# A gated mix of a state-space convolution and a Fourier filter: one of the sine products moves to GpSimd, its sign is turned back at an eviction, and responses are stored eight channels at a time

## The chip, the cores and the metric

One core of a Trainium2 chip runs the whole kernel in one launch. The metric is the device time of that launch in microseconds; the median of three runs stands for the kernel. The profile shows one further execution, instruction by instruction.

## The reference

The input x has 2048 positions and 640 channels. Branch A is a long convolution: each channel has a response K of 2048 values, a sum over 128 decaying complex exponentials, and the convolution is done with transforms of twice the length. Branch B filters the same x with a two-dimensional real Fourier transform. A sigmoid gate mixes them.

```python
def _A_ref(u, log_A_real, A_imag, C_real, C_imag, log_dt, D_skip):
    dt = jnp.exp(log_dt)
    A = -jnp.exp(log_A_real) + 1j * A_imag
    C = (C_real + 1j * C_imag) * dt[:, None]
    P = jnp.exp((A * dt[:, None])[:, :, None] * pos[None, None, :])
    K = 2.0 * jnp.einsum("dn,dnl->dl", C, P).real
    ...                                   # y = irfft(rfft(u, 2L) * rfft(K, 2L))[:L]
    return y + u * D_skip[None, None, :]

def _B_ref(x, w_r, w_i):
    X = jnp.fft.rfft2(x, axes=(-2, -1))
    X = X * (w_r + 1j * w_i)
    return jnp.fft.irfft2(X, s=(S, D), axes=(-2, -1))

g = sigmoid((x * gate_w).sum(-1, keepdims=True))
return g * _A_ref(...) + (1 - g) * _B_ref(...)
```

## The kernel before

Two streams of work are written side by side by `merge` and then ordered for each engine by a scheduler; on an engine the order is fixed before the launch, and each engine runs its own list in order, waiting on semaphores. The first stream (`phase_a`) transforms x along the positions (lines L335, L348, until about 160 us), then does the Fourier filter of branch B, called FNet below: nine blocks of rows, each of which goes through `front` (tiles ue, fo, fg), transposes (p_t), matmuls (p_d), the filter `filt` on VectorE (tiles xx, mm, zz, pm) and two back transforms (p_eo, p_i). After it `phase_c` starts the transform of the responses, `first`.

The second stream is `phase_b`. It makes the responses K, in 40 tiles of 16 channels (four blocks of 40 groups of four channels). For a tile t:

- `mags` makes e, the magnitudes: three matmuls p_e (L638) and three exponentials on ScalarE (L640), 128 x 1536.
- `phases` makes q, the angles, 128 x 1024: two matmuls p_p (L649), a copy on ScalarE (L651) and a subtraction on VectorE (L652). The first 512 of them belong to x, the last 512 to y.
- `trig` takes the magnitude of the angles, aq (VectorE, L662), and four sines on ScalarE: sc holds both of y's, in SBUF; sx and cx are x's sine and cosine, in PSUM.
- `prods` multiplies. x[:, 1] is e times sx, near half (32 positions, L676) and far half with a minus sign (L675); x[:, 0] is e times cx for both halves (L677, 1024 wide). All three run on VectorE and read e from SBUF and the sines from PSUM. y's two products (L679, L680) run on GpSimd and read SBUF alone, the only memory that GpSimd works on here.
- `kgen` multiplies y by x on TensorE: 32 small matmuls p_k (L693). After every second tile the eight channels in p_k are copied by ScalarE into kt (L701); after ten tiles one store takes kt's 40 columns to k_d (L703).

Exponentials and sines come in turns of five tiles (BT = 5), since ScalarE changes its tables between them. I call the stretches Exp stage and Sin stage; there are eight of each. Tiles q, aq and sc come from one pool of five buffers, b_w; sx and cx have one PSUM bank each. `prods(t)` is written behind `trig(t + 1)`, and `kgen(t)` some two tiles later. A buffer's next writer waits for the last reader of what it held.

The transformed x goes to DRAM (u_d) from ut, a pool of four, and FNet reads it back (ue). Stores and loads on SP, ScalarE's queue (ACTq) and GpSimd are issued in order on each of them. `first` (L750 and the copy it hands to `stage1`) reads k_d back and transforms it; `phase_d` multiplies, transforms back and writes out, from about 438 us on.

Of the kernel before, what the change touches and what calls it, by code (L numbers as in the profile page):

```python
# [9 lines left out]
F32 = mybir.dt.float32  # L10
# [3 lines left out]
ALU = mybir.AluOpType  # L14
# [36 lines left out]
def _tables():  # L51
# [19 lines left out]
    for r in range(4):  # L71
# [5 lines left out]
        np.full((128, 1), HALF_PI)], 1)  # L77
# [106 lines left out]
def body(tc, A, out):  # L184
    nc = tc.nc
    T = Ctx()
    with ExitStack() as top:
# [19 lines left out]
        T.sg = [take(1), take(1)]  # L207
        T.hpi = take(1)
# [392 lines left out]
def phase_b(tc, A, T, ctx):  # L601
# [5 lines left out]
    wt = ctx.enter_context(tc.tile_pool(name="b_w", reuse_waits="tile", bufs=5))  # L607
# [5 lines left out]
    pt = ctx.enter_context(tc.tile_pool(name="b_pt", reuse_waits="tile", bufs=1, space=PSUM))  # L613
# [41 lines left out]
    def trig(t, r):  # L655

        aq = wt.tile([128, 2, 16, 32], F32, tag="w", name="aq")
        sc = r.sc = wt.tile([128, 2, 16, 32], F32, tag="w", name="sc")
        sx, cx = r.sx, r.cx = [pt.tile([128, 16, 32], F32, tag=n, name=n) for n in ("sx", "cx")]
        fl = lambda t: t.rearrange("p d i -> p (d i)")  # L660
        af = aq.rearrange("p v d i -> p (v d i)")
        V.tensor_scalar(out=af.bitcast(I32), in0=r.q.bitcast(I32), scalar1=0x7FFFFFFF, scalar2=None, op0=ALU.bitwise_and)  # L662

        with after(st.exp):
            S.activation(fl(sc[:, 0]), r.q[:, 512:1024], AF.Sin, scale=TWO_PI)  # L665
        S.activation(fl(sc[:, 1]), af[:, 512:1024], AF.Sin, scale=-TWO_PI, bias=T.hpi)  # L666
        S.activation(fl(sx), r.q[:, 0:512], AF.Sin, scale=TWO_PI)
        T.trig = st.trig = S.activation(fl(cx), af[:, 0:512], AF.Sin, scale=-TWO_PI, bias=T.hpi)  # L668

    def prods(t, r):  # L670
        e, sx, cx, sc = es[t], r.sx, r.cx, r.sc
        x = wk.tile([128, 2, 16, 64], F32, tag="x", name="x")
        y = wk.tile([128, 2, 16, 32], F32, tag="y", name="y")
        xy[t] = (x, y)
        V.scalar_tensor_tensor(out=x[:, 1, :, 32:64], in0=e[:, :, 32:64], scalar=-1.0, in1=sx[:, :, :], op0=ALU.mult, op1=ALU.mult)  # L675
        V.tensor_tensor(out=x[:, 1, :, 0:32], in0=e[:, :, 0:32], in1=sx[:, :, :], op=ALU.mult)  # L676
        V.tensor_tensor(out=x[:, 0].rearrange("p d (h j) -> p d h j", h=2), in0=e[:, :, 0:64].rearrange("p d (h j) -> p d h j", h=2),  # L677
                        in1=cx.unsqueeze(2).broadcast_to([128, 16, 2, 32]), op=ALU.mult)
        G.tensor_tensor(out=y[:, 1], in0=e[:, :, 64:96], in1=sc[:, 0], op=ALU.mult)  # L679
        G.tensor_tensor(out=y[:, 0], in0=e[:, :, 64:96], in1=sc[:, 1], op=ALU.mult)  # L680

    def kgen(t):
        x, y = xy.pop(t)
        if t % 10 == 0:
            st.kt = w1.tile([128, 40, 64], F32, tag="k", name="kt")
        kt = st.kt
# [47 lines left out]
def phase_c(tc, A, T, ctx):  # L734
# [243 lines left out]
```

## Time and profile before

| | us |
|---|---|
| median of three runs | 609.23 (608.76 to 611.23) |
| the profiled execution's own time | 608.74 |
| its span, first to last instruction | 607.0 |
| TensorE busy | 535.8 (88%) |
| VectorE busy | 500.2 (82%) |
| ScalarE busy | 364.8 (60%) |
| GpSimd busy | 267.0 (44%) |

By stretches of the span, busy us of each engine:

| stretch | TensorE | VectorE | ScalarE | GpSimd |
|---|---|---|---|---|
| 0 to 53: first transforms of x, parameters | 43.49 | 34.95 | 28.90 | 28.88 |
| 53 to 160: more of them, beside ten tiles of responses | 98.07 | 78.69 | 73.29 | 33.44 |
| 160 to 438: FNet beside thirty tiles | 249.45 | 251.59 | 220.80 | 121.56 |
| 438 to 607: products with the responses, output | 144.81 | 134.97 | 41.85 | 83.11 |

A row of the profile names the line of the kernel, the engine (PE is TensorE, DVE VectorE, ACT ScalarE, POOL GpSimd, SPq SyncE's queue), the operation and the tiles, out<-in. Busy time is the time in which an engine had an instruction in work; a recorded instruction can contain waiting for the memory port.

### The profile page before, as it was taken

What the parts mean: (1) busy time and instruction counts of PE and PEld (TensorE: products, weight loads), DVE (VectorE), ACT (ScalarE), POOL (GpSimd) and SP (SyncE); (2) the same over time, 40 slices, a digit from 0 to 9 for tenths busy, and PEclk for the clock granted to TensorE, in tenths of its full rate; (3) what the DMA queues carried; (4) which work ended last, traced back from release to release, by engine and by line L of the source; (5) the groups of instructions that cost most, each with busy time, mean ns of one, the idle gap of its engine ahead of it and who ended that gap; (6) DMA issues with size and microseconds to landing.
All of it is one profiled execution on the core that took longest, in us unless ns stands there. A gap on an engine that the chain in (4) does not pass through costs nothing.

```text
span 607.0 us, 16654 instructions
## 1 busy us (share of the span) xinstructions
PE 535.8 (88%) x7084; PEld 405.6 (67%) x7084; DVE 500.2 (82%) x748; ACT 364.8 (60%) x659; POOL 267.0 (44%) x246
## 2 busy tenths in 40 slices
PE   9688979989968989989798999898989999999874
PEld 7576657766656657676566676565878877787631
DVE  5971597598899989999999899979399796987974
ACT  4556775576846876888589888799723332231210
POOL 4931252053525344454326335416254347547441
PEclk9899989989989996998899999999999999999998
DMA  8787204245612320332250233006685989889776
GB/s 341 293 288 268 79 5 151 69 154 181 239 43 67 97 87 13 108 118 109 67 151 12 75 97 110 24 28 200 224 346 184 356 273 299 291 271 310 225 231 239
DMA packets 48083, 101.98 MB, mean 168 GB/s; under 512 B 3316, under 2 KB 32776, under 8 KB 46248
## 3 DMA queue, kind: packets, MB, share of 16 engines
q1 hardware_dynamic: 24888, 67.74, 32.3%
q10 hardware_dynamic: 20080, 22.52, 11.9%
q0 software_dynamic: 3040, 10.65, 5.3%
q8 instruction: 56, 0.92, 0.6%
q14 instruction: 19, 0.16, 0.1%
HBM read 60.91 MB, written 39.98 MB: 166 GB/s over the span
## 4 chain that ended last, share of the span: by engine, by line
PE 51%; DVE 27%; ACT 9%; DMA 8%; issue 4%; POOL 1%; ACTq 0%; DVEq 0%; POOLq 0%; SPq 0%
PE p_eo L551 8%; PE p_s L348 8%; PE p_s L335 6%; PE p_e L638 5%; PE p_k L693 4%; PE p_i L814 4%; PE p_p L649 3%; DVE q L652 3%; PE p_d L518 2%; DVE t L801 2%; PE p_i L565 2%; PE p_t L502 2%; DVE ma L795 2%; PE p_c L893 2%; PE p_d L519 2%
## 5 line engine op out<-in xcount | busy, mean ns | idle before, releaser
L679 POOL TENSOR_TENSOR y<-e,sc 128x512 f32<-128x512 f32 x40 | 56.7, 1418 | 131.0 <-ACT sc L665 60.3
L348 PE MATMUL p_s<-t,w 128*64 128x160 f32 x1056 | 92.4, 314 | 10.2 <-ACT ut L382 5.1
L348 PEld LDWEIGHTS p_s<-t,w 128*64 128x64 f32 x1056 | 76.5, 139 | 21.4 <-ACT ut L382 6.0
L640 ACT ACTIVATE e<-p_e 128x512 f32<-128x512 f32 x120 | 68.6, 602 | 22.7 <-PE p_e L638 20.4
L551 PE MATMUL p_eo<-td,pmt 107*128 107x321 f32 x204 | 69.0, 459 | 3.9 <-ACT pmt L505 3.9
L693 PE MATMUL p_k<-x,y 128*32 128x64 f32 x2560 | 63.6, 229 | 9.8 <-DVE x L677 2.9
L693 PEld LDWEIGHTS p_k<-x,y 128*32 128x32 f32 x2560 | 46.1, 113 | 38.0 <-issue 29.4
L652 DVE SCALAR_TENSOR_TENSOR q<-q,p_p 128x512 f32<-128x512 f32 x80 | 53.4, 681 | 13.5 <-ACT q L651 11.8
L336 ACT COPY t<-p_s 128x512 f32<-128x512 f32 x40 | 24.6, 623 | 65.2 <-PE p_s L335 41.8
L638 PE MATMUL p_e<-rm,par 128*128 128x512 f32 x120 | 58.7, 519 | 3.4 <-ACT e L640 2.8
L680 POOL TENSOR_TENSOR y<-e,sc 128x512 f32<-128x512 f32 x40 | 54.5, 1362 | 6.5 <-ACT sc L666 6.5
L800 POOL TENSOR_TENSOR t<-ma 64x320 f32<-64x320 f32 x32 | 28.0, 875 | 61.4 <-DVE ma L795 51.8
L551 PEld LDWEIGHTS p_eo<-td,pmt 107*128 107x128 f32 x204 | 38.4, 198 | 19.6 <-ACT pmt L505 6.9
L677 DVE TENSOR_TENSOR x<-e,cx 128x1024 f32<-128x1024 f32 x40 | 48.6, 1214 | 2.2 <-ACT cx L668 2.2
L651 ACT ACTIVATE q<-p_p 128x512 f32<-128x512 f32 x80 | 46.5, 592 | 4.2 <-PE p_p L649 3.8
L649 PE MATMUL p_p<-rp,par 128*128 128x512 f32 x80 | 43.5, 548 | 4.5 <-DVE q L652 4.5
L814 PE MATMUL p_i<-t,w 128*64 128x160 f32 x528 | 42.7, 300 | 4.4 <-POOL t L801 3.4
L335 PE MATMUL p_s<-c,kt 128*64 128x128 f32 x640 | 43.0, 274 | 3.9 <-DVE mb L796 2.0
L335 PEld LDWEIGHTS p_s<-c,kt 128*64 128x64 f32 x640 | 38.0, 136 | 12.6 <-issue 7.7
L816 ACT COPY s<-p_i 128x640 f32<-128x640 f32 x32 | 21.8, 694 | 40.0 <-PE p_i L814 30.4
L335 PE MATMUL p_s<-c,u 128*64 128x128 f32 x640 | 41.5, 278 | 2.5 <-ACT ut L382 2.5
L795 DVE TENSOR_TENSOR ma<-p_s,us 128x640 f32<-128x640 f32 (+1 forms) x36 | 28.2, 784 | 18.8 <-PE p_s L348 11.5
(153 smaller groups left out, 1181.5 us busy)
## 6 DMA issues: line engine op xcount, KB each, us to landing
u_d<-ut SPq DMA_DIRECT2D x32, 320.0 KB, 2.6
us<-u_d ACTq DMA_DIRECT2D x16, 640.0 KB, 6.0
s_d<-s ACTq DMA_DIRECT2D x15, 640.0 KB, 8.3
t<-s_d SPq DMA_DIRECT2D x14, 640.0 KB, 5.9
ww<-in_w_l SPq DMA_DIRECT2D x8, 642.0 KB, 4.0
ue<-u_d SPq DMA_DIRECT2D x8, 640.0 KB, 4.4
k_d<-kt SPq DMA_DIRECT2D x4, 1280.0 KB, 7.6
kt<-k_d SPq DMA_DIRECT2D x8, 640.0 KB, 5.9
```

Source lines behind the costliest of these rows:

```text
L335: nc.tensor.matmul(p[64 * ri:64 * ri + 64, j, :], src(i + j), e1[ri], start=True, stop=True)
L348: ins = nc.tensor.matmul(p[64 * j:64 * j + 64, i, 160 * ri:160 * ri + 160], w2[:, x, 64 * ri:64 * ri + 64], t1[:, x // 2 if x < 32 else K0 ...
L551: P.matmul(p[:, :E], st.pmt[:DC, c, w, j, :], tv[:DC, w, c, :], start=c == 0, stop=c == 2)
L638: P.matmul(p[:, :], pars[t], rm[:, c:c + 512], start=True, stop=True)
L640: st.exp = S.activation(ef[:, c:c + 512], p[:, :], AF.Exp)
L649: P.matmul(p[:, :], pars[t], rp[:, c:c + 512], start=True, stop=True)
L652: V.scalar_tensor_tensor(out=qf[:, c:c + 512], in0=qf[:, c:c + 512], scalar=MAGIC, in1=p[:, :], op0=ALU.subtract, op1=ALU.subtract)
L677: V.tensor_tensor(out=x[:, 0].rearrange("p d (h j) -> p d h j", h=2), in0=e[:, :, 0:64].rearrange("p d (h j) -> p d h j", h=2), in1=cx.uns ...
L679: G.tensor_tensor(out=y[:, 1], in0=e[:, :, 64:96], in1=sc[:, 0], op=ALU.mult)
L680: G.tensor_tensor(out=y[:, 0], in0=e[:, :, 64:96], in1=sc[:, 1], op=ALU.mult)
L693: P.matmul(st.pb[32 * r:32 * r + 32, o, :], y[:, ri, 4 * qq + JR[r], :], x[:, ri, 4 * qq + JR[r], :], start=t % 2 + qq + 1 - ri == 0, stop ...
L814: T.mm = P.matmul(p[x:x + 64, i // 2, 160 * (i % 2):160 * (i % 2) + 160], T.w3[:, k0 + h + i, x:x + 64], t2[:, h + i, :], start=True, stop ...
```

## The change

x's two halves trade engines and signs. Its product with the sine, x[:, 1], is now one operation of 1024 elements on GpSimd, without the minus sign; its product with the cosine, x[:, 0], is two operations of 512 on VectorE, the far half with a minus sign. The response of the far half therefore comes out negated, and `near` turns it back: the eviction in `first` on ScalarE multiplies by T.sa, a column of 1 and -1. Since GpSimd reads no PSUM here, the sine must lie in SBUF: the sines are written over the angles (q) and over their magnitudes (aq), in place, and sc and sx go away. So all four sines come behind aq, which reads q; before, the two that read q directly did not. The pool b_w has six buffers, two for a tile in place of three; cx has two PSUM banks. kt holds eight columns, has two buffers, and is stored after every second tile: 20 stores of 512 columns in place of four of 2560.

```diff
@@ -74,7 +74,7 @@
     c1 = np.concatenate([
         e1[0], e1[1], e3.reshape(4, 32, 64).swapaxes(0, 1).reshape(128, 64), e3e.reshape(128, 128), np.eye(128), one,
         np.repeat([-1.0, 1.0], 64)[:, None], np.repeat([1.0, -1.0], 64)[:, None],
-        np.full((128, 1), HALF_PI)], 1)
+        np.tile(np.repeat([1.0, -1.0], 32), 2)[:, None], np.full((128, 1), HALF_PI)], 1)
 
     k = np.array(POS_K)
     a = np.arange(64)
@@ -205,6 +205,7 @@
         T.e1 = [take(128), take(128)]
         T.e3, T.e3e, T.id, T.one = take(64), take(128), take(128), take(32)
         T.sg = [take(1), take(1)]
+        T.sa = take(1)
         T.hpi = take(1)
         T.w2 = cst.tile([128, NP, 128], F32, name="w2")
         T.gate = cst.tile([128, 2, 16], F32, name="gate")
@@ -604,13 +605,13 @@
     V, G, S, P = nc.vector, nc.gpsimd, nc.scalar, nc.tensor
     BT = 5
     ep = ctx.enter_context(tc.tile_pool(name="b_e", reuse_waits="tile", bufs=BT))
-    wt = ctx.enter_context(tc.tile_pool(name="b_w", reuse_waits="tile", bufs=5))
+    wt = ctx.enter_context(tc.tile_pool(name="b_w", reuse_waits="tile", bufs=6))
     wk = ctx.enter_context(tc.tile_pool(name="b_x", reuse_waits="tile", bufs=3))
     w2 = ctx.enter_context(tc.tile_pool(name="b_p", reuse_waits="tile", bufs=2))
     w1 = ctx.enter_context(tc.tile_pool(name="b_k", reuse_waits="tile", bufs=1))
     ps = ctx.enter_context(tc.tile_pool(name="b_ps", reuse_waits="tile", bufs=2, space=PSUM))
     pk = ctx.enter_context(tc.tile_pool(name="b_pk", reuse_waits="tile", bufs=1, space=PSUM))
-    pt = ctx.enter_context(tc.tile_pool(name="b_pt", reuse_waits="tile", bufs=1, space=PSUM))
+    pt = ctx.enter_context(tc.tile_pool(name="b_pt", reuse_waits="tile", bufs=2, space=PSUM))
     rp, rm = T.rp, T.rm
     dsk = w1.tile([128, 4, 40], F32, name="dsk")
     V.memset(dsk[:, :, :], 0.0)
@@ -654,36 +655,33 @@
 
     def trig(t, r):
 
-        aq = wt.tile([128, 2, 16, 32], F32, tag="w", name="aq")
-        sc = r.sc = wt.tile([128, 2, 16, 32], F32, tag="w", name="sc")
-        sx, cx = r.sx, r.cx = [pt.tile([128, 16, 32], F32, tag=n, name=n) for n in ("sx", "cx")]
+        aq = r.aq = wt.tile([128, 2, 16, 32], F32, tag="w", name="aq")
+        cx = r.cx = pt.tile([128, 16, 32], F32, tag="cx", name="cx")
         fl = lambda t: t.rearrange("p d i -> p (d i)")
         af = aq.rearrange("p v d i -> p (v d i)")
         V.tensor_scalar(out=af.bitcast(I32), in0=r.q.bitcast(I32), scalar1=0x7FFFFFFF, scalar2=None, op0=ALU.bitwise_and)
-
         with after(st.exp):
-            S.activation(fl(sc[:, 0]), r.q[:, 512:1024], AF.Sin, scale=TWO_PI)
-        S.activation(fl(sc[:, 1]), af[:, 512:1024], AF.Sin, scale=-TWO_PI, bias=T.hpi)
-        S.activation(fl(sx), r.q[:, 0:512], AF.Sin, scale=TWO_PI)
-        T.trig = st.trig = S.activation(fl(cx), af[:, 0:512], AF.Sin, scale=-TWO_PI, bias=T.hpi)
+            S.activation(r.q[:, 512:1024], r.q[:, 512:1024], AF.Sin, scale=TWO_PI)
+        S.activation(r.q[:, 0:512], r.q[:, 0:512], AF.Sin, scale=TWO_PI)
+        S.activation(fl(cx), af[:, 0:512], AF.Sin, scale=-TWO_PI, bias=T.hpi)
+        T.trig = st.trig = S.activation(af[:, 512:1024], af[:, 512:1024], AF.Sin, scale=-TWO_PI, bias=T.hpi)
 
     def prods(t, r):
-        e, sx, cx, sc = es[t], r.sx, r.cx, r.sc
+        e, cx = es[t], r.cx
+        si = r.q.rearrange("p (v d i) -> p v d i", v=2, d=16)
         x = wk.tile([128, 2, 16, 64], F32, tag="x", name="x")
         y = wk.tile([128, 2, 16, 32], F32, tag="y", name="y")
         xy[t] = (x, y)
-        V.scalar_tensor_tensor(out=x[:, 1, :, 32:64], in0=e[:, :, 32:64], scalar=-1.0, in1=sx[:, :, :], op0=ALU.mult, op1=ALU.mult)
-        V.tensor_tensor(out=x[:, 1, :, 0:32], in0=e[:, :, 0:32], in1=sx[:, :, :], op=ALU.mult)
-        V.tensor_tensor(out=x[:, 0].rearrange("p d (h j) -> p d h j", h=2), in0=e[:, :, 0:64].rearrange("p d (h j) -> p d h j", h=2),
-                        in1=cx.unsqueeze(2).broadcast_to([128, 16, 2, 32]), op=ALU.mult)
-        G.tensor_tensor(out=y[:, 1], in0=e[:, :, 64:96], in1=sc[:, 0], op=ALU.mult)
-        G.tensor_tensor(out=y[:, 0], in0=e[:, :, 64:96], in1=sc[:, 1], op=ALU.mult)
+
+        V.tensor_tensor(out=x[:, 0, :, 0:32], in0=e[:, :, 0:32], in1=cx[:, :, :], op=ALU.mult)
+        V.scalar_tensor_tensor(out=x[:, 0, :, 32:64], in0=e[:, :, 32:64], scalar=-1.0, in1=cx[:, :, :], op0=ALU.mult, op1=ALU.mult)
+        G.tensor_tensor(out=y[:, 1], in0=e[:, :, 64:96], in1=si[:, 1], op=ALU.mult)
+        G.tensor_tensor(out=x[:, 1].rearrange("p d (h j) -> p d h j", h=2), in0=e[:, :, 0:64].rearrange("p d (h j) -> p d h j", h=2),
+                        in1=si[:, 0].unsqueeze(2).broadcast_to([128, 16, 2, 32]), op=ALU.mult)
+        G.tensor_tensor(out=y[:, 0], in0=e[:, :, 64:96], in1=r.aq[:, 1], op=ALU.mult)
 
     def kgen(t):
         x, y = xy.pop(t)
-        if t % 10 == 0:
-            st.kt = w1.tile([128, 40, 64], F32, tag="k", name="kt")
-        kt = st.kt
         if t % 2 == 0:
             st.pb = pk.tile([128, 8, 64], F32, tag="pk", name="p_k")
         for qq in range(4):
@@ -698,9 +696,9 @@
 
             for r in range(4):
                 P.matmul(st.pb[32 * r:32 * r + 32, :, 31], T.id[:, 32 * r:32 * r + 32], dsk[:, c, i:i + 8], start=False, stop=True)
-            S.copy(kt[:, i:i + 8, :], st.pb[:, :, :])
-            if t % 10 == 9:
-                nc.sync.dma_start(T.k_d[c], kt[:, :, :])
+            kt = w2.tile([128, 8, 64], F32, tag="k", name="kt")
+            S.copy(kt[:, :, :], st.pb[:, :, :])
+            nc.sync.dma_start(T.k_d[c, :, i:i + 8], kt[:, :, :])
 
     def run():
         pend = []
@@ -749,11 +747,15 @@
             T.kt[c, h] = T.kp.tile([128, 20, 64], F32, tag="k", name="kt")
             T.ki[c, h] = nc.sync.dma_start(T.kt[c, h][:, :, :], T.k_d[c, :, 20 * h:20 * h + 20])
 
+    def near(dst, src):
+
+        S.activation(dst, src, AF.Copy, scale=T.sa)
+
     def first(c, ps):
         t1 = T.t1[c] = T.tp[c % 2].tile([128, 16, 160, 2], F32, tag="t1", name="t1")
         t1v = t1.rearrange("p x d y -> p d x y")
         for h in range(2):
-            yield from stage1(nc, ps, T.e1, lambda q: T.kt[c, h][:, q, :], 20, t1v[:, 80 * h:80 * h + 80], S.copy)
+            yield from stage1(nc, ps, T.e1, lambda q: T.kt[c, h][:, q, :], 20, t1v[:, 80 * h:80 * h + 80], near)
             load_k(c + 1, h)
 
     T.load_k, T.first = load_k, first
```

What it does to the order shows on three engines. GpSimd, the tiles of the Sin stage from 361 to 390 us; y, x, e are one tile's products and magnitudes, numbered by buffer. Before:

```order
L679 TENSOR_TENSOR y_4521<-e_4253,sc_4480 128x512
L680 TENSOR_TENSOR y_4521<-e_4253,sc_4480 128x512
L679 TENSOR_TENSOR y_4573<-e_4313,sc_4512 128x512
L680 TENSOR_TENSOR y_4573<-e_4313,sc_4512 128x512
L679 TENSOR_TENSOR y_4648<-e_4402,sc_4564 128x512
L680 TENSOR_TENSOR y_4648<-e_4402,sc_4564 128x512
```

The same three tiles on GpSimd now:

```order
L678 TENSOR_TENSOR y_4480<-e_4214,q_4425 128x512
L679 TENSOR_TENSOR x_4479<-e_4214,q_4425 128x1024
L681 TENSOR_TENSOR y_4480<-e_4214,aq_4442 128x512
L678 TENSOR_TENSOR y_4530<-e_4276,q_4449 128x512
L679 TENSOR_TENSOR x_4529<-e_4276,q_4449 128x1024
L681 TENSOR_TENSOR y_4530<-e_4276,aq_4472 128x512
L678 TENSOR_TENSOR y_4604<-e_4365,q_4486 128x512
L679 TENSOR_TENSOR x_4603<-e_4365,q_4486 128x1024
L681 TENSOR_TENSOR y_4604<-e_4365,aq_4522 128x512
```

Each tile has a third, wider product between its two.

TensorE in the same stage, the second of those tiles; p_p are the angles of later tiles, p_t FNet's transposes. Before:

```order
L502 MATMUL p_t_4726<-c1_65,fg_4547 128x64 x4
L693 MATMUL p_k_4655<-x_4572,y_4573 32x64 x12
L649 MATMUL p_p_4695<-rp_74,par_3899 128x512
L693 MATMUL p_k_4655<-x_4572,y_4573 32x64 x20
L502 MATMUL p_t_4780<-c1_65,fg_4547 65x64 x3
L649 MATMUL p_p_4700<-rp_74,par_3899 128x512
```

The same place on TensorE now:

```order
L650 MATMUL p_p_4650<-rp_74,par_3868 128x512
L552 MATMUL p_eo_4646<-td_2001,pmt_4455 128x321
L650 MATMUL p_p_4655<-rp_74,par_3868 128x512
L691 MATMUL p_k_4610<-x_4529,y_4530 32x64 x5
L503 MATMUL p_t_4675<-c1_65,fg_4506 128x64 x4
L691 MATMUL p_k_4610<-x_4529,y_4530 32x64 x8
L503 MATMUL p_t_4681<-c1_65,fg_4506 128x64 x4
L691 MATMUL p_k_4610<-x_4529,y_4530 32x64 x19
```

The tile's matmuls stay beside the same transposes, and the angles of the stage's last tile now come ahead of them.

SP's queue around 90 to 160 us, stores of x's transform (u_d), of responses (k_d), and FNet's first loads. Before:

```order
L430 DMA u_d<-ut 128x640 x8
L430 DMA u_d<-ut 64x320
L473 DMA w_2018<-in_t_w 128x256
L473 DMA w_2139<-in_t_w 128x256
L453 DMA td<-in_t_td 128x3213
L430 DMA u_d<-ut 128x640
L475 DMA ue<-u_d 128x4x320
```

SP's queue now, at the same place:

```order
L431 DMA u_d<-ut 128x640
L701 DMA k_d<-kt 128x512
L431 DMA u_d<-ut 128x640 x7
L474 DMA w_2003<-in_t_w 128x256
L431 DMA u_d<-ut 64x320
L474 DMA w_2126<-in_t_w 128x256
L701 DMA k_d<-kt 128x512
L454 DMA td<-in_t_td 128x3213
L701 DMA k_d<-kt 128x512
L431 DMA u_d<-ut 128x640
L476 DMA ue<-u_d 128x4x320
```

Stores of responses stand between and ahead of u_d's stores, where before the first came only behind them.

## The prediction

> **What bounds the kernel now.** I read the 40 slices first: VectorE's digits stand at 9 from a quarter of the span to two thirds of it, where TensorE's fall to 8. The borders of the stages I took from the timeline of the response tiles (exponentials of five tiles, then sines of five), and asked for each engine's busy time between them. Columns: stretch and length, then TensorE, weight loads, VectorE, ScalarE, GpSimd, the granted clock, DMA share, GB/s.
>
> ```profile
> 70.00:96.00 26.00, 21.95 (x445) 15.85 (x441) 23.66 (x37) 19.09 (x34) 16.80 (x13) 0.93 0.18 53
> ...
> 116.00:144.00 28.00, 25.34 (x509) 18.72 (x505) 25.36 (x42) 18.80 (x33) 13.38 (x11) 0.94 0.42 144
> ...
> 160.00:200.00 40.00, 32.14 (x343) 24.82 (x341) 40.00 (x57) 25.40 (x47) 20.99 (x19) 0.91 0.26 89
> 200.00:221.00 21.00, 20.79 (x200) 14.11 (x197) 18.44 (x31) 15.30 (x29) 5.78 (x4) 1.00 0.35 104
> 221.00:250.00 29.00, 25.82 (x274) 19.11 (x276) 26.77 (x38) 23.32 (x44) 15.06 (x12) 0.82 0.20 61
> ...
> 269.00:300.00 31.00, 25.71 (x373) 18.89 (x371) 29.35 (x40) 22.48 (x41) 14.06 (x11) 0.94 0.29 100
> ...
> 318.00:343.00 25.00, 22.63 (x352) 17.06 (x351) 24.27 (x39) 23.08 (x44) 15.50 (x15) 1.00 0.22 58
> ...
> 361.00:390.00 29.00, 24.71 (x371) 16.99 (x370) 27.08 (x39) 22.05 (x43) 14.59 (x10) 1.00 0.23 76
> ...
> 406.00:438.00 32.00, 28.95 (x611) 21.88 (x609) 22.27 (x33) 28.05 (x54) 15.00 (x13) 1.00 0.52 175
> ```
>
> The stretch 200:221 is an Exp stage: TensorE is full (20.79 of 21). The other eight are the Sin stages, 240 us together with 207.25 of TensorE in them. There VectorE is fullest nearly everywhere (40.00 of 40, 24.27 of 25), and TensorE idles 32.75 us. That is the most the change can win; after 438 us nothing but the eviction through `near` is touched.
>
> **VectorE's saving.** The names are those of the code: x and y the products, e the exponentials, q and aq the phase and its magnitude, fo, mm, zz and pm FNet's. Groups of the stretch 150:430 (thirty tiles, beside the FNet row blocks); the last numbers are busy us and mean ns of one.
>
> ```profile
> L677 DVE TENSOR_TENSOR x<-e,cx 128x1024 f32<-128x1024 f32 x30 | 36.4, 1213 | 2.2 <-ACT cx L668 2.2
> L662 DVE TENSOR_SCALAR aq<-q 128x1024 int32<-128x1024 int32 x30 | 23.8, 794 | 0.1
> L676 DVE TENSOR_TENSOR x<-e,sx 128x512 f32<-128x512 f32 x30 | 20.4, 678 | 0.0
> ...
> L482 DVE TENSOR_TENSOR fo<-ue 128x640 f32<-128x640 f32 x8 | 8.8, 1095 | 0.0
> L536 DVE TENSOR_TENSOR mm<-xx,ww 128x642 f32<-128x642 f32 x8 | 8.3, 1036 | 0.0
> ...
> L541 DVE TENSOR_TENSOR pm<-zz 128x642 f32<-128x642 f32 x8 | 7.7, 960 | 0.0
> L533 DVE TENSOR_TENSOR mm<-xx,ww 128x642 f32<-128x642 f32 x8 | 7.6, 954 | 0.0
> ...
> L542 DVE TENSOR_TENSOR pm<-zz 128x642 f32<-128x642 f32 x8 | 7.3, 906 | 0.0
> L532 DVE TENSOR_TENSOR mm<-xx,ww 128x642 f32<-128x642 f32 x8 | 7.2, 905 | 0.0
> ...
> L537 DVE TENSOR_TENSOR mm<-xx,ww 128x642 f32<-128x642 f32 x8 | 6.5, 818 | 0.0
> L538 DVE TENSOR_TENSOR zz<-mm 128x321 f32<-128x321 f32 x8 | 6.1, 761 | 0.0
> L539 DVE TENSOR_TENSOR zz<-mm 128x321 f32<-128x321 f32 x8 | 6.0, 752 | 0.0
> L535 DVE TENSOR_TENSOR zz<-mm 128x321 f32<-128x321 f32 x8 | 4.6, 578 | 0.0
> ...
> L539 DVE TENSOR_TENSOR zz<-mm 64x321 f32<-64x321 f32 x1 | 0.5, 478 | 0.0
> ```
>
> The two 512-wide products with cx cost what those with sx did (L676, 678 ns, same operands from SBUF and PSUM), so VectorE loses exactly L677: 1.213 us per tile, 36.4 us over the thirty.
>
> **GpSimd's load.** The new product is 1024 wide. The nearest rows of GpSimd with two inputs in SBUF are the additions of the output:
>
> ```profile
> L899 POOL TENSOR_TENSOR ot<-ot,oe 128x480 f32<-128x480 f32 x12 | 14.4, 1228 | 6.2 <-issue 6.0
> ...
> L899 POOL TENSOR_TENSOR ot<-ot,oe 128x320 f32<-128x320 f32 x5 | 4.3, 870 | 0.9 <-DVE ot L898 0.9
> ```
>
> Their slope is 358 ns for 160 elements, so 870 + 704 x 2.24 = 2.45 us. The lower end is 2.33, with the slope from the 320-wide row to an undisturbed 512-wide y (1.27 us, further down: 400 ns for 192); the upper 3.0, if each waits for VectorE as long as the y quoted next (1.83 for 1.27). I take 2.45, the row without VectorE beside it being the nearer. A tile then holds GpSimd 1.27 + 2.45 + 1.27 = 5.0 us in place of 2.5.
>
> **What the two engines take from each other.** An undisturbed aq and one that met a y (GpSimd's y began first):
>
> ```profile
> L662 DVE TENSOR_SCALAR aq<-q x40: 677/687/1753, 72.2 to 426.6; 128x1024 int32<-128x1024 int32 x40
> ...
> 228.53 1.75 DVE L662 TENSOR_SCALAR aq<-q 128x1024 int32<-128x1024 int32 x1
> ```
> ```profile
> 227.91 1.83 POOL L679 TENSOR_TENSOR y<-e,sc 128x512 f32<-128x512 f32 x1
> ```
>
> aq ends 0.5 us after y with its whole work behind it: it waited 1.06 us. The groups above tell the same. Against the undisturbed 818 (642 wide) and 478 ns (321 wide), the eight rows from L482 to L535 without L537 are longer by 277 + 218 + 142 + 136 + 88 + 87 and, for the narrow ones, 283 + 274 + 100: 1605 ns, x8 = 12.8 us; aq adds 30 x (794 - 687) = 3.2. So 16 us of VectorE's stretch are waits behind GpSimd. Operations with one input in PSUM (L676) show none.
>
> How does that grow? An operation that arrives at random meets one of GpSimd's in proportion to its length and waits half of it: the square. Per tile that is 2 x 1.27 squared = 3.2 now, and 3.2 + 2.45 squared = 9.2 afterwards, 2.8 times. 16 becomes 45 us, and of the 36.4 us only about 7.5 are left. If it grew with busy time alone (2 times), 20 would be left; that is the other end.
>
> [...]
>
> In the two Sin stages ahead of 150 VectorE has no FNet work; there TensorE idles 4.05 + 2.66 us only, and the tiles' pace will be GpSimd's (below): I count nothing for them.
>
> **GpSimd late for TensorE.** GpSimd's first product of four tiles, and TensorE's first matmul on each:
>
> ```profile
> 363.28 1.27 POOL L679 TENSOR_TENSOR y<-e,sc 128x512 f32<-128x512 f32 x1 [7.28 <-ACT sc L665]
> ...
> 368.73 1.28 POOL L679 TENSOR_TENSOR y<-e,sc 128x512 f32<-128x512 f32 x1 [2.36 <-ACT sc L665]
> ...
> 374.38 1.28 POOL L679 TENSOR_TENSOR y<-e,sc 128x512 f32<-128x512 f32 x1 [2.53 <-ACT sc L665]
> ...
> 380.56 1.27 POOL L679 TENSOR_TENSOR y<-e,sc 128x512 f32<-128x512 f32 x1 [3.64 <-issue]
> ```
> ```profile
> 370.28 0.31 PE L693 MATMUL p_k<-x,y 128*32 128x64 f32 x6
> ...
> 375.73 0.54 PE L693 MATMUL p_k<-x,y 128*32 128x64 f32 x24
> ...
> 380.93 0.30 PE L693 MATMUL p_k<-x,y 128*32 128x64 f32 x2
> ...
> 389.27 0.32 PE L693 MATMUL p_k<-x,y 128*32 128x64 f32 x8
> ```
>
> Tiles come every 5.2 to 6.2 us. Afterwards one takes GpSimd 5.0, plus aq's 0.69 in which it can't start, plus FNet's two-input operations (about 0.7 by this stage's share): 6.4. All sines now wait for aq, since they overwrite q: the first y starts 0.69 later, at 364.0. Tiles are done at 370.4, 376.8, 383.2, 389.6, against 370.3, 375.7, 380.9, 389.3: up to 2.3 us late, and TensorE works in order, so FNet's matmuls and the next exponentials behind p_k wait too. The listing gives p_k nearly the same places. For the five stages with tiles this close (70, 116, 318, 361, 406; ahead of 160 the pace without FNet is 5.7 against 4.8, about 3.5 late) I take 2.3, 3.5, 2.3, 2.3, and 2.6 for the last, in which GpSimd also issues FNet's last stores: 13 us. In the stages at 160, 221 and 269 there is room:
>
> ```profile
> 271.48 1.27 POOL L679 TENSOR_TENSOR y<-e,sc 128x512 f32<-128x512 f32 x1 [4.46 <-ACT sc L665]
> ```
> ```profile
> 281.75 0.30 PE L693 MATMUL p_k<-x,y 128*32 128x64 f32 x2
> ```
>
> 10 us from y to p_k; nothing is counted.
>
> **The small edits.** Sixteen more k_d stores on SP: the responses are first read where SP issues this load, which waits for FNet, so zero.
>
> ```profile
> 419.91 11.74 SPq L750 DMA_DIRECT2D kt<-k_d  x3
> ```
>
> Without that cover, u_d stores that now stand behind a k_d store wait for p_k and ScalarE's copy, by 0 to the 3.5 us of above at each of the three places where that happens; ut is four deep, so I take 0. cx in two buffers frees ScalarE from VectorE's x: inside the saving already. `near` in place of a copy: ScalarE has 41.85 us of work in the 169 us after 438, so even a few us more are hidden.
>
> ```profile
> 438.00:607.00 169.00, 144.81 (x1728) 113.38 (x1728) 134.97 (x199) 41.85 (x68) 83.11 (x89) 0.99 0.83 277
> ```
>
> **Sum**, against the profiled execution's 608.7 us (0.5 under the median of the runs shown): 608.7 - 7.5 + 13 = 614.2; as a median 614.
>
> **Rivals.** Faster: the waits grow with busy time only and GpSimd's lag is taken up by the sixth tile (angles three tiles deep) before p_k. VectorE nets 20 us, of which the Sin stages, with 26 us of TensorE's idle time after 160, give perhaps two thirds: -13, 596. It decides where the 1024-wide product takes the lower 2.33 us and p_k, in the same places, finds its tiles ready. Chance 0.30. Cancelling: lateness of 8 in place of 13, 609; 0.20.
>
> The port fills: six Sin stages after 160 (to 432) last 180 us; the tiles alone ask 30 x 5.7 = 171 us of the place where both engines meet, the nine row blocks 9 x 6.8 = 61 us (six 642-wide and four 321-wide), even over the 278 us 40 of them here: 31 us too much. Exp stages take a third: +21, 630. Against it: y's hold looks shorter than its record. [...] My forecast 0.36.
>
> Half a per cent (3 us) is what a measurement tells from no change. Faster 0.30, same 0.20, slower 0.50. Own range of the forecast 612 to 621; for all cases 596 to 631.
>
> **What the new profile would show.** VectorE's count falls by 40, but L536, L538 and aq are longer than 1036, 761 and 794 ns. GpSimd's x takes 2.3 to 3.0 us and GpSimd is over 90% busy in the Sin stages; TensorE waits at p_k for y and x from GpSimd, and the Exp stage after is still full. I am wrong if two-input operations keep their lengths, or if p_k's waits stay under 5 us in all.

## The result, and the profile after

The changed kernel takes 662.7 us (median of six runs, 662.0 to 665.6) against 609.0 for the kernel before beside it (606.8 to 614.6): a ratio of 1.088, interval 1.083 to 1.093. I had said 614, and no more than 631. The profiled execution took 665.6 us. In the table of the experiments the times are medians of all executions, while the ratios to before leave out the few that ran slow (two of four in a5, one of four in d2, three of ten in b2, two of seven in g1).

Two stretches divide each kernel at its last sine: first before, then after. Columns: stretch and length, then busy us of TensorE, weight loads, VectorE, ScalarE, GpSimd, the granted clock, DMA share, GB/s.

```profile
0.00:428.90 428.90, 382.35 (x5120) 284.72 (x5122) 363.73 (x548) 315.86 (x579) 181.71 (x156) 0.96 0.37 124
428.90:607.00 178.10, 153.46 (x1968) 120.91 (x1964) 136.48 (x201) 48.98 (x81) 85.27 (x91) 0.99 0.82 274
```
```profile
0.00:485.60 485.60, 408.00 (x5123) 302.95 (x5124) 368.43 (x507) 315.08 (x579) 269.24 (x195) 0.89 0.33 110
485.60:663.90 178.30, 153.51 (x1966) 120.65 (x1962) 136.63 (x201) 52.92 (x81) 86.79 (x92) 0.98 0.80 272
```

All 56.7 us lie ahead of the last sine; behind it nothing changed. The row divides them: TensorE does the same matmuls (5123 for 5120) and is busy 25.7 us longer with them, at a clock of 0.89 in place of 0.96, and it idles 77.6 us in place of 46.55, 31.05 more. That is bookkeeping: no run shows how much of the 25.7 us would have been idle time at a full clock. By stages, the eight Sin stages take 245.3 us together in place of 231.9, the eight Exp stages 182.7 in place of 140.4: TensorE does in the Exp stages (busy 38 us more) what it didn't get to in the Sin stages (13 us less). VectorE was to have 48.5 us less work (40 times 1.213) and is busy 4.7 us longer.

The groups of after up to the last sine (engine, tiles, busy us, mean ns, idle time just before and its end):

```profile
L679 POOL TENSOR_TENSOR x<-e,q 128x1024 f32<-128x1024 f32 x40 | 101.6, 2540 | 0.0
L681 POOL TENSOR_TENSOR y<-e,aq 128x512 f32<-128x512 f32 x40 | 58.9, 1473 | 0.1
L678 POOL TENSOR_TENSOR y<-e,q 128x512 f32<-128x512 f32 x40 | 52.7, 1317 | 111.1 <-ACT q L664 72.5 <-issue 37.9 <-POOL y L681 0.6
```
```profile
L662 DVE TENSOR_SCALAR aq<-q 128x1024 int32<-128x1024 int32 x40 | 52.6, 1315 | 0.6
L676 DVE TENSOR_TENSOR x<-e,cx 128x512 f32<-128x512 f32 x40 | 27.2, 679 | 11.2 <-ACT cx L666 11.1
...
L538 DVE TENSOR_TENSOR mm<-xx,ww 128x642 f32<-128x642 f32 x8 | 10.7, 1342 | 0.0
```

x takes 2.54 us on GpSimd, within the range that I gave; aq, 0.69 undisturbed, has a mean of 1.32, since sixteen of the forty take more than 1 us. The x products with a PSUM operand (L676) still take 679 ns. A tile holds GpSimd 5.3 us (2.54 + 1.47 + 1.32), and in the Sin stages it is busy 203 of 245 us by eight rows like these two, the third and the fourth of them:

```profile
184.20:217.20 33.00, 28.34 (x306) 19.52 (x306) 29.25 (x36) 20.39 (x37) 26.14 (x18) 0.74 0.13 39
242.60:274.40 31.80, 19.06 (x273) 14.42 (x274) 28.25 (x31) 21.26 (x40) 26.33 (x18) 0.81 0.22 65
```

What is waited for there is in the list of waits (us in total, times, longest):

```profile
ACT q L664 <- DVE aq L662: 38.1, 15, 5.6
```
```profile
PE p_k L691 <- POOL x L679: 20.7, 10, 5.0
PE p_eo L552 <- ACT pmt L506: 12.4, 4, 5.3
PE p_k L691 <- POOL y L681: 7.2, 6, 1.6
```

Before, ScalarE's sines waited for VectorE too, the first for q itself and the second for aq, 25.8 us together, and TensorE hardly waited at p_k for GpSimd:

```profile
ACT sc L665 <- DVE q L652: 18.3, 14, 2.4
ACT sc L666 <- DVE aq L662: 7.5, 5, 2.5
```
```profile
PE p_k L693 <- POOL y L680: 2.0, 1, 2.0
```

I read a ring from this: GpSimd's products hold aq on VectorE, all four sines wait for aq, the next products on GpSimd wait for the sines, and TensorE, whose list is in order, waits at p_k for GpSimd and keeps the next tile's angles behind it (ScalarE's copies of angles waited 13.0 us for them, before 3.8). One turn of it, GpSimd, VectorE, ScalarE:

```profile
96.52 1.28 POOL L678 TENSOR_TENSOR y<-e,q 128x512 f32<-128x512 f32 x1
97.76 2.36 POOL L679 TENSOR_TENSOR x<-e,q 128x1024 f32<-128x1024 f32 x1
100.08 1.25 POOL L681 TENSOR_TENSOR y<-e,aq 128x512 f32<-128x512 f32 x1
102.69 1.28 POOL L678 TENSOR_TENSOR y<-e,q 128x512 f32<-128x512 f32 x1 [1.36 <-ACT q L664]
```
```profile
97.29 4.60 DVE L662 TENSOR_SCALAR aq<-q 128x1024 int32<-128x1024 int32 x1
101.81 1.27 DVE L383 COPY ut<-p_s 128x320 f32<-128x320 f32 x3
```
```profile
101.92 0.63 ACT L664 ACTIVATE q<-q 128x512 f32<-128x512 f32 x1 [5.61 <-DVE aq L662]
```

aq starts while a y is at work. It does not get through when that y ends at 97.80, nor when x ends at 100.12: it ends at 101.89, 0.56 us after the last y. Here it waits for a whole row of GpSimd's back-to-back operations, with three copies of VectorE's behind it and ScalarE idle for 5.61 us: GpSimd's next instruction came first again, twice.

That is the longest kind of wait, not the common one. Of the sixteen long aq, three wait out more than one operation of GpSimd (those from 97.29, 208.64 and 321.68 us). The other thirteen come in behind one, and where GpSimd's next one stands right behind that, it waits in its turn (the next y took 1.70 to 1.73 us four times, the next x 2.83 twice), as here, VectorE first:

```profile
423.57 2.88 DVE L662 TENSOR_SCALAR aq<-q 128x1024 int32<-128x1024 int32 x1
```
```profile
423.53 2.37 POOL L679 TENSOR_TENSOR x<-e,q 128x1024 f32<-128x1024 f32 x1
425.86 1.72 POOL L681 TENSOR_TENSOR y<-e,aq 128x512 f32<-128x512 f32 x1
```

aq ends at 426.45, 0.55 us after x, and the y behind x takes 1.72 us in place of 1.28.

Then the clock. It changes on a grid: every stretch of one clock that the trace records ahead of the last sine lasts a whole number of 3.41 us. Windows of that length, columns as above:

```profile
422.92:426.33 3.41, 2.82 (x83) 2.00 (x81) 3.41 (x3) 1.83 (x4) 3.41 (x3) 1.00 0.00 0
426.33:429.74 3.41, 0.94 (x5) 0.49 (x5) 3.41 (x8) 3.26 (x7) 3.41 (x3) 1.00 0.00 0
429.74:433.16 3.42, 3.23 (x12) 2.81 (x13) 1.95 (x4) 1.68 (x5) 3.08 (x2) 0.50 0.23 78
433.16:436.57 3.41, 3.41 (x12) 2.24 (x11) 1.28 (x2) 3.38 (x6) 3.12 (x2) 0.50 0.01 3
436.57:439.98 3.41, 3.41 (x71) 2.70 (x70) 0.88 (x2) 1.19 (x3) 1.67 (x2) 0.50 0.00 0
```

In the second window TensorE works 0.94 us of 3.41, and for the next three it is granted half its clock although it is full. Each of the fifteen half-speed stretches ahead of the last sine begins after such a window, with TensorE busy in at most 53% of it. Not every such window brings one: of the seventeen at full clock, fifteen did, and one of the seven stretches of before came after a window that was 61% busy. The fifteen last 109 us together; those of before, 37.5.

### The profile page after: what moved, and what is told of

The parts are those of the page before. It is cut to its first block, busy times and chain, and to the rows that moved or that the text cites. A ratio compares the mean times of both kernels' runs of the same rounds, so it can differ in the third digit from the quotient of the medians.

```text
span 663.9 us, 16742 instructions
## 1 busy us (share of the span) xinstructions
PE 561.5 (85%) x7084; PEld 423.6 (64%) x7084; DVE 505.1 (76%) x708; ACT 368.0 (55%) x659; POOL 356.0 (54%) x286
## 5 line engine op out<-in xcount | busy, mean ns | idle before, releaser
L678 POOL TENSOR_TENSOR y<-e,q 128x512 f32<-128x512 f32 x40 | 52.7, 1317 | 111.1 <-ACT q L664 72.5
L349 PE MATMUL p_s<-t,w 128*64 128x160 f32 x1056 | 96.0, 317 | 13.9 <-ACT ut L383 6.1
L679 POOL TENSOR_TENSOR x<-e,q 128x1024 f32<-128x1024 f32 x40 | 101.6, 2540 | 0.0
L691 PE MATMUL p_k<-x,y 128*32 128x64 f32 x2560 | 67.7, 239 | 29.9 <-POOL x L679 20.7
L552 PE MATMUL p_eo<-td,pmt 107*128 107x321 f32 x204 | 77.9, 502 | 12.4 <-ACT pmt L506 12.4
L752 ACT ACTIVATE t<-p_s,c 128x512 f32<-128x512 f32 x40 | 28.6, 721 | 64.9 <-PE p_s L336 43.6
L552 PEld LDWEIGHTS p_eo<-td,pmt 107*128 107x128 f32 x204 | 42.7, 219 | 29.4 <-ACT pmt L506 14.9
L681 POOL TENSOR_TENSOR y<-e,aq 128x512 f32<-128x512 f32 x40 | 58.9, 1473 | 0.1
L662 DVE TENSOR_SCALAR aq<-q 128x1024 int32<-128x1024 int32 x40 | 52.6, 1315 | 0.6
L664 ACT ACTIVATE q<-q 128x512 f32<-128x512 f32 x40 | 25.1, 627 | 38.3 <-DVE aq L662 38.1
```

The source lines that it names most:

```text
L349: ins = nc.tensor.matmul(p[64 * j:64 * j + 64, i, 160 * ri:160 * ri + 160], w2[:, x, 64 * ri:64 * ri + 64], t1[:, x // 2 if x < 32 else K0 ...
L552: P.matmul(p[:, :E], st.pmt[:DC, c, w, j, :], tv[:DC, w, c, :], start=c == 0, stop=c == 2)
L678: G.tensor_tensor(out=y[:, 1], in0=e[:, :, 64:96], in1=si[:, 1], op=ALU.mult)
L679: G.tensor_tensor(out=x[:, 1].rearrange("p d (h j) -> p d h j", h=2), in0=e[:, :, 0:64].rearrange("p d (h j) -> p d h j", h=2), in1=si[:, ...
L681: G.tensor_tensor(out=y[:, 0], in0=e[:, :, 64:96], in1=r.aq[:, 1], op=ALU.mult)
L691: P.matmul(st.pb[32 * r:32 * r + 32, o, :], y[:, ri, 4 * qq + JR[r], :], x[:, ri, 4 * qq + JR[r], :], start=t % 2 + qq + 1 - ri == 0, stop ...
```

## The experiments

Theory: GpSimd's product costs by holding VectorE, aq above all, and the sines behind it. Rivals: TensorE waits for a late x; the sines in place, all behind aq, cost by themselves; the stores cost. "TensorE" below is its busy and its idle time up to the last sine, from the same kind of row as above (before: 382 and 47; after: 408 and 78).

| run | what | us | ratio to before | TensorE |
|---|---|---|---|---|
| a1 | after, product on VectorE | 640.9 | 1.053 (1.047 to 1.059) | 393, 66 |
| a2 | after, product left out | 618.9 | 1.016 (1.009 to 1.023) | 395, 45 |
| a3 | after, product not read | 662.5 | 1.089 (1.083 to 1.095) | 406, 74 |
| a4 | after, aq on ScalarE | 676.7 | 1.112 (1.106 to 1.117) | 408, 87 |
| a5 | after, sines of q in own tile | 664.6 | 1.086 (1.076 to 1.095) | 403, 75 |
| a8 | after, aq split | 663.8 | 1.096 (1.088 to 1.105) | 406, 72 |
| d1 | a5, product on VectorE | 622.9 | 1.027 (1.019 to 1.036) | 381, 57 |
| d2 | a5, product left out | 601.4 | 0.989 (0.982 to 0.996) | 372, 43 |
| b1 | before, product added, not read | 662.7 | 1.089 (1.082 to 1.095) | 400, 81 |
| b2 | before, six buffers and stores | 611.9 | 0.999 (0.993 to 1.004) | 382, 48 |
| e1 | a8, aq in PSUM | 655.9 | 1.077 (1.072 to 1.083) | 406, 65 |
| e2 | a5, half of the product each | 647.7 | 1.065 (1.056 to 1.074) | 396, 68 |
| e3 | e1, product left out | 601.1 | 0.988 (0.980 to 0.995) | 375, 43 |
| e4 | e1, product last and not read | 627.4 | 1.031 (1.024 to 1.038) | 387, 58 |
| a3b | a8, product last and not read | 657.4 | 1.081 (1.072 to 1.089) | 399, 72 |
| f3 | a8, useless matmuls | 679.4 | 1.116 (1.108 to 1.123) | 421, 76 |
| g1 | before, aq in PSUM | 639.8 | 1.049 (1.044 to 1.054) | |

**The product back on VectorE (a1).** `G.tensor_tensor(out=x[:, 1]` becomes `V.tensor_tensor(out=x[:, 1]`.

> The changed kernel with one thing undone: x's sine product goes back to VectorE, as one operation of 1024 on the sine in SBUF. In place sines, six buffers, eight-channel stores and the sign at the eviction stay. If GpSimd's product is the cause of the 54 us, in whatever way, this gives 603 to 615 us. If the sines written in place (all four behind aq) or the stores are the cause, it stays above 640.

641, by a hair in the second range. But 22 us come back and 32 stay, so neither the product nor the rest makes the loss alone in this order of the work.

**The product left out (a2).** The same line is taken out, and p_k reads `x[:, 0, ...]` for both.

> The changed kernel with x's sine product left out altogether (TensorE multiplies y by x[:, 0] in both of its places; the output is not the reference's). This is the ceiling: 2.5 us of GpSimd and 1.2 us of VectorE fewer per tile than in any version that works. All theories of the product say 590 to 605 us; in-place sines or stores as the cause would keep it above 635.

619: above the ceiling of the theories of the product, and under the 635 of the others. TensorE's idle time is that of before (45 for 47 us), but it is busy 12 us longer, and its half-speed stretches come to 78.5 us for 37.5. ScalarE's list has changed too. One Sin stage of before, of after (a2's list has the same lumps), and of a5, worked out from the lists (q: a copy of angles, two to a tile; S: a sine, four to a tile; K: a copy of p_k):

```
before  qqSSSSqqSSqSSqSSqSSqSKSqSSqSSSS
after   qqqqSSSSSSSSqqKSSSSqqqSSSSqSSSS
a5      qqSSSSqqSSqSSqSKSqSSqSSqSSqSSSS
```

With all sines behind one aq, the scheduler puts the angles of two tiles first and then eight sines in a row. I had shown the lists of GpSimd, TensorE and SP, not this one.

**The product not read (a3).** p_k reads `x[:, 0, ...]` for both; GpSimd still makes x[:, 1], between its two y.

> The changed kernel, in which GpSimd makes x[:, 1] as before but TensorE reads x[:, 0] in its place (the output is not the reference's): the product still meets VectorE at the memory, but nothing on TensorE waits for it; y's second product still stands behind it on GpSimd. If what costs is VectorE held off by GpSimd (aq and FNet's two-input operations, and the sines behind aq), it stays at 650 to 665. If what costs is TensorE waiting at p_k for a late x (16.8 us of recorded waits, and the clock that falls behind them), it comes to 610 to 630.

662.5, in the range of VectorE held off, and as with the product read: TensorE's wait for x itself is not needed for the loss. It then waits for the y that stands behind x on GpSimd (17.8 us), which this run leaves in.

**aq on ScalarE (a4).**

```diff
-        V.tensor_scalar(out=af.bitcast(I32), in0=r.q.bitcast(I32), scalar1=0x7FFFFFFF, ...)
+        with after(st.exp):
+            S.activation(af, r.q, AF.Abs)
```

> The changed kernel with aq made by ScalarE (absolute value, 1024 wide, one operation of about 1.1 us) in place of VectorE: aq can no longer be held off by GpSimd, and the sines no longer wait for VectorE there. ScalarE has 5.5 us more in each Sin stage. If the chain aq held off, sines late, GpSimd late is the cause, most comes back: 610 to 630. If TensorE's waits at p_k for a GpSimd that is too slow are the cause, it stays at 650 to 665.

677, slower still, outside both. ScalarE has 1.06 us more per tile, ahead of every sine, and still waited 51 us for q from VectorE. It tells nothing about the hold by itself.

**Sines of q in a tile of their own (a5), aq split (a8).**

```diff
-            S.activation(r.q[:, 512:1024], r.q[:, 512:1024], AF.Sin, scale=TWO_PI)
+            S.activation(s[:, 512:1024], r.q[:, 512:1024], AF.Sin, scale=TWO_PI)
```
```diff
+        for v in (1, 0):
+            h = slice(512 * v, 512 * v + 512)
+            V.tensor_scalar(out=af[:, h].bitcast(I32), in0=r.q[:, h].bitcast(I32), ...)
```

> The changed kernel with the sines of q written into a tile of their own (four buffers for q and aq, two for it), so that they need not stand behind aq. ScalarE's list then reads one pair of sines, one copy of angles, and so on, as before the change; the changed kernel's list has the angles of two tiles and then eight sines in a row. GpSimd's product stays. If the lumps of two tiles cost half of it (the run with the product back on VectorE, lumps and all, was still 5% slower than before): 625 to 640. If GpSimd's product alone makes it, in any order: 650 to 665.

> The changed kernel with aq made in two operations of 512, y's half first, sines still in place: each half's sines stand behind half an aq, and ScalarE's list comes out interleaved as before the change. VectorE has 40 more operations, each half as long. If the lumps are the cause of half the loss: 625 to 640; if it is the writing in place with its wait for aq, or GpSimd's product in any order: 650 to 665.

664 and 664, by the ratios 1.086 and 1.096 beside the change's 1.088, both in the second range. With GpSimd's product there, the lumps and the writing in place make no clear difference.

**The same without GpSimd's product (d1, d2).** a5 with the edits of a1 and of a2.

> Sines of q in a tile of their own, and x's sine product back on VectorE (one operation of 1024, two operands in SBUF): neither lumps nor a 1024-wide GpSimd product are left of the change; the stores of eight channels and the sign at the eviction are. If these two make all of the 54 us: 600 to 612. If stores, sign or six buffers cost anything, it stays at 620 or more.

> Sines of q in a tile of their own and x's sine product left out (TensorE reads x[:, 0] twice; the output is not the reference's): the ceiling without lumps. VectorE and GpSimd both have less to do than before the change, so 590 to 602 if VectorE was what bound the Sin stages; 605 to 612 if saving VectorE's time gains nothing even when nobody pays for it.

623 and 601: by the ratios 2.6 and 2.7% less than a1 and a2, some 16 us each. So all four sines behind one aq, with the lumps that come of it, did cost 16 us, but only where GpSimd did not cost more. The writing in place by itself does not: e3 below keeps it, with aq in halves, and is as fast as d2. d2 is the ceiling without lumps: with 41 us less VectorE time ahead of the last sine than before (and no product for anyone), it gains 1.1%, some 7 us. Its 601 lies at the upper end of the range that I had given for VectorE as the bound, and by the ratio (602) on its edge; but a gain of 7 for 41, with TensorE's idle time at 43 for 47 us, reads as a load that bound little. d1 lies in its second range, though stores and buffers are not the reason, as b2 below shows. It does on VectorE what before does, but takes the sine from SBUF, not PSUM. The product then has a mean of 1470 ns (L677 of before took 1213), which fits its meeting y's; that this makes the whole 21 us between d1 and d2 isn't shown.

**The product added to the kernel before (b1), and its control (b2).**

```diff
+        xn = w1.tile([128, 16, 64], F32, tag="xn", name="xn")
+        G.tensor_tensor(out=xn.rearrange(...), in0=e[:, :, 0:64].rearrange(...), in1=sc[:, 0].unsqueeze(2)..., op=ALU.mult)
```

> The kernel before with eight-channel stores, to which a 1024-wide product on GpSimd is added for every tile, behind both of y's, into a tile that nobody reads. VectorE, TensorE and ScalarE keep all their work, sines in their own tiles, and the order of their lists. If GpSimd's product costs by holding VectorE off: 640 to 665. If it costs only because TensorE waits for what stands on GpSimd: y's products are ahead of it, so at most the next tile's y is late, 607 to 620.

> The kernel before with only the sixth buffer and the eight-channel stores: the control of the run with the extra product. 604 to 611 if they cost nothing, as I took; 615 or more if sixteen more stores on SP delay FNet's.

The control equals before (0.999). b1 is the clearest of all: 663, as slow as the change, with VectorE's, ScalarE's and TensorE's work and ScalarE's order unchanged, nothing in place, and nobody reading the product. So the product on GpSimd is enough for the whole loss. By which way is not settled here: TensorE still waits 12.3 us at p_k for a y, which stands behind the last tile's product. Its row for VectorE's aq, and its stretch to the last sine:

```profile
L662 DVE TENSOR_SCALAR aq<-q 128x1024 int32<-128x1024 int32 x40 | 57.4, 1434 | 0.3
```
```profile
0.00:481.40 481.40, 400.43 (x5120) 296.48 (x5122) 408.51 (x548) 316.30 (x579) 279.86 (x195) 0.91 0.34 113
```

VectorE is busy 408.5 us for 363.7: 45 us more in the same 548 instructions, which fits their waiting behind GpSimd.

**aq into PSUM (e1).**

```diff
+            ap = pt.tile([128, 512], F32, tag="ap", name="ap")
+            V.tensor_scalar(out=ap.bitcast(I32), in0=r.q[:, h].bitcast(I32), ...)
...
+            S.activation(af[:, h] if v else fl(cx), ap[:, :], AF.Sin, scale=-TWO_PI, bias=T.hpi)
```

> The changed kernel with aq made in two halves into PSUM, from where ScalarE takes its cosines (cx has one bank then): a VectorE operation with its output in PSUM should not have to wait for GpSimd, but takes about 0.68 us for each 512 (1.4 a tile in place of 0.7, 27 us more of VectorE). If aq held off by GpSimd, and the sines behind it, is what costs: 620 to 645 in spite of the added work. If GpSimd's pace or FNet's two-input operations cost it: 655 to 680.

```profile
L665 DVE TENSOR_SCALAR ap<-q x80: 677/694/696, 75.4 to 468.6; 128x512 int32<-128x512 int32 x80
```
```profile
PE p_k L692 <- POOL x L680: 23.4, 16, 4.7
```

The hold is gone: of 80 operations beside GpSimd's products none took over 0.70 us (in SBUF one took 4.87). Yet only 8 us come back (1.077 for a8's 1.096), at the edge of the rival's range; TensorE now waits 23 us at p_k for x. ap has one bank, in which VectorE waits 20 us for ScalarE; without the product the same bank costs nothing (e3).

**Half of the product on each engine (e2).**

```diff
+        V.tensor_tensor(out=x[:, 1, :, 32:64], in0=e[:, :, 32:64], in1=si[:, 0], op=ALU.mult)
+        G.tensor_tensor(out=x[:, 1, :, 0:32], in0=e[:, :, 0:32], in1=si[:, 0], op=ALU.mult)
```

> Sines of q in a tile of their own, and x's sine product divided: the near half (512) on GpSimd, the far half on VectorE. GpSimd has 3.7 us a tile in place of 5.0. With the product on VectorE it was 623, on GpSimd 664. If the loss goes with what GpSimd holds, in proportion: 640 to 646. If it goes with the square of one operation's length: 628 to 636. If it comes from GpSimd's 5 us against a tile's pace of 5.2 to 6.2, it is gone: 612 to 624.

648, a little over the proportional case. With GpSimd at 3.7 us a tile the loss is not gone, so its 5 us against the tiles' pace are no threshold.

**Hold and lateness apart (e3, e4, a3b).** e1 without the product; e1 with it behind both y and not read; a8 with it behind both y and not read.

> aq in halves into PSUM as in the run before, and x's sine product left out altogether (TensorE reads x[:, 0] twice; not the reference's output): the control for the next run. With sines in their own tile and aq in SBUF the same omission gave 601; 27 us more VectorE work should cost some of its spare time only: 603 to 625.

> aq in PSUM, and GpSimd's x product behind both of y's and read by nobody (TensorE reads x[:, 0] twice; not the reference's output): neither is aq held nor does TensorE wait for the product. If the hold on aq and the late x are two causes of which each is enough: within 15 us of the control without a product, 610 to 635. If GpSimd's occupation itself (the next tile's y behind it) or FNet's held operations make the loss: 640 to 656.

> aq split in SBUF (as in the run with the split aq, 664), GpSimd's x product behind both of y's and read by nobody (TensorE reads x[:, 0] twice; not the reference's output): aq is held as before, but TensorE waits for nothing behind the product. If the hold on VectorE is enough: 645 to 664. If the lateness of x and of the y behind it is what costs: 610 to 635.

| ratio to before | TensorE waits for the product | it does not |
|---|---|---|
| aq can be held | 1.096 (a8) | 1.081 (a3b) |
| aq cannot | 1.077 (e1) | 1.031 (e4) |
| no product | | 0.988 (e3), 0.989 (d2) |

e3 came out under its range, a3b in its first. e4 is in the first range as a time, but 26 us above its control, not within 15. Over e4 the lateness adds 4.7% of before, the hold on aq 5.0%, both together 6.6%, not 9.7: they overlap, and whichever one takes away, most of the loss stays. The two are not wholly apart: in a3b TensorE waits no longer for the product, but 15 us at p_k for y, and the intervals of a8 and a3b overlap. The 4.3% between e4 and no product (26 us) are in all four. In e4 FNet's L533 has a mean of 2.53 us (median 0.82, longest 6.32), which fits FNet's two-input operations being held; I took away neither that by itself nor GpSimd's being occupied when the next y comes, so this part stays open.

In what VectorE does, e3 and d2 differ by aq's form alone (where the sines are written, and ScalarE's list, differ too). d2, then e3:

```profile
0.00:414.20 414.20, 371.60 (x5054) 280.29 (x5056) 322.92 (x507) 313.68 (x579) 178.07 (x156) 0.97 0.38 128
```
```profile
0.00:417.90 417.90, 375.00 (x5102) 277.15 (x5104) 336.78 (x547) 312.38 (x580) 171.84 (x157) 0.98 0.39 130
```

VectorE is busy 14 us longer in e3 and the time is the same: here VectorE's load is no bound. At the load of before only g1 asks that, without an answer.

**Gaps filled with useless matmuls (f3).** a8, with four bf16 matmuls of 512 columns of zeros ahead of a tile's p_k, and eight of 256 ahead of every second tile's:

```diff
+        for n in range(4 if t % 2 == 0 else 8):
+            P.matmul(st.pb[:, 0:w]..., zl[:, 0:128], zl[:, 0:64 * w], ...)
```

> [...] If TensorE's gaps bring its clock down and that makes half the loss, busy gaps keep it up: 645 to 664 in spite of the added work. If the clock falls for another reason: 680 to 700.

```profile
L694 PE MATMUL p_k<-zl 128*128 128x512 bf16 x76 | 25.1, 450 | 5.7 <-ACT kt L708 5.5
L694 PE MATMUL p_k<-zl 128*128 128x256 bf16 x152 | 23.8, 298 | 0.0
```

679, between the two ranges. How long such matmuls take, no run had shown; up to the last sine the zeros have 48.9 us of TensorE's busy time, partly over that of other matmuls. Without the zeros TensorE is busy 382.7 us, 23.6 less than in a8 (406.3), and its half-speed stretches come to 85.3 us for 105.8. That agrees with a clock that follows the gaps; since the lists moved too, it is not proof, and it did not pay.

**aq into PSUM in the kernel before (g1).** y's magnitude in the bank that sx takes afterwards, x's in that of cx.

> The kernel before (all of x's products on VectorE with sines in PSUM, y's on GpSimd) with one thing from the experiments: aq in two halves into PSUM, y's in the bank that then takes sx, x's in the bank of cx, turned to the cosine in place. aq can't be held off by GpSimd; VectorE has 27 us more work. If holds on aq (3.5 us in the kernel before) and VectorE's load matter little, it is within 1% of before, 600 to 614; if the meetings that are left in the kernel before cost through the sines, 592 to 602; if VectorE's load bounds after all, 620 to 635.

640, outside all three ranges. By its place in the code, sharing a bank makes each tile's magnitude wait until the last tile's sx is used, so VectorE's load and this wait aren't told apart: inconclusive.

## Why the prediction was wrong, step by step

- **What bounds the kernel** failed first. I took VectorE's fullness in the Sin stages (40.00 of 40) for the bound and made the change's worth VectorE's saving less its waits. d2 saves 41 us of VectorE's busy time ahead of the last sine (363.7 to 322.9), pays nothing, and gains 7; e3 gives 14 of them back at no cost. So little of a net saving on VectorE, my 7.5 us or the rival's 20, could reach the time, and VectorE's balance (+4.7 us busy) tells nothing of the 54. What sets the pace instead fits the tile's chain of angles, aq, sines, products and p_k, which the hold lengthens at one end and the late products at the other; that the chain is the bound is argued from the waits, not shown by a run.
- **The square rule** was too low as VectorE's ledger, but of the right order: 48.5 us less work and 4.7 more busy make 53 us of new waits over forty tiles, 1.3 us a tile; I had 29 over thirty, 1.0 a tile. (The rows that I called eight are nine; their sum holds.) Of the three operations that I named, aq went from 767 to 1315 ns over forty tiles, the mm of old L536 from 1036 to 1078, and the zz of old L538 from 761 to 654; others went up in its stead (mm of old L537 from 818 to 1342). What failed is the place: I booked aq's wait as VectorE's time, 3.2 us grown 2.8 times over thirty tiles or 0.3 us each, while it comes to 0.6 us each and stands ahead of four sines, up to 4.87 us for one aq, and ScalarE waited 38.1 us for it.
- **GpSimd late for TensorE** was the term of 13 us. TensorE's idle time grew by 31, and its waits at p_k for GpSimd alone came to 27.9. I followed single tiles with the sines only 0.69 us later; in a ring the delay of one tile is the start of the next. With one half of the ring cut (e1, a3b) most of the loss stays, with both (e4) a third of it.
- **The clock** was no term at all: the same matmuls took 25.7 us longer, beside 31 of idle time. The row 221:250 of before, granted 0.82, had shown the effect, and the prediction says nothing of it.
- **The order.** I wrote that the list gives p_k nearly the same places; ScalarE's list had moved to lumps of two tiles. It costs 16 us where GpSimd's product does not cover it, and nothing beside it.
- **The small edits** at nothing: right (b2, 0.999). `near` has a mean of 721 ns for the copy's 624, and the part behind the last sine kept its length.
- **The marks:** VectorE's count fell by 40, x took 2.54 us, TensorE waited at p_k for x and y (27.9 us): right. The Exp stage is still full: right (24.20 of 24.20 us from 436.4 on), and all eight are longer together, since TensorE does there what waited. GpSimd over 90% busy in the Sin stages: wrong, 83%, since it too waits, for the sines.
- **The rivals:** "the port fills", 630, had the mechanism nearest to what was seen (VectorE held while GpSimd works, one aq for 4.87 us), but as a sum of work that overfills one place. By the records of both engines that place, GpSimd's operations and VectorE's between SBUF and SBUF taken together, is occupied in 216 of the Sin stages' 245 us (before, 153 of 232): near full, not full. And with aq out of it (e1) little comes back. I gave it 0.14.

## What to carry to other kernels

A full engine is not yet the bound: ask what the time does if its work vanishes, and whether the operation you slow stands at the head of a chain. Before work goes to GpSimd, look for VectorE operations between SBUF and SBUF that others wait for; reading from PSUM (x, a mean of 679 ns with GpSimd's product and of 678 without) or writing to it (half an aq, at most 0.70 us in e1, up to 2.56 in SBUF in a8) kept them out of its way here. Where a wait of TensorE empties half of a 3.41 us window, reckon with slower matmuls behind it too: after fifteen of seventeen such windows here the clock was halved.

## What was not expected of the hardware

- A held VectorE operation can wait for a back-to-back row of GpSimd's, not for one alone: 4.60 us through a y, x and y. It was so for three of the sixteen aq over 1 us.
- The same operation with its output in PSUM was never held: 80 times at most 0.70 us (e1), where the same halves in SBUF took up to 2.56 (a8). So where VectorE writes decides here whether it is held; by what mechanism, no run shows. It is also slower: 512 elements take 0.69 us in the median, as long as an undisturbed 1024 from SBUF to SBUF.
- Half-speed stretches of TensorE's clock went from 37.5 to 109 us without more work on it.
